# A fused attention and FFT kernel: another list of seeds for its planner, so another order on every engine

## The chip, the cores and the metric

The kernel runs on one core of a Trainium2 chip. A core has five engines that work side by side, each through its own queue in order: TensorE (PE, matrix products; its weight loads are the rows PEld), VectorE (DVE), ScalarE (ACT), GpSimd (POOL) and SyncE (SP, which here issues DMAs only). ACT and POOL issue DMAs too. The engines wait for each other through semaphores. The metric is the device time of one execution in microseconds (us); lower is better.

## The reference

Two branches read the same input x of 2048 rows by 640 and are mixed by a gate of one number per row.

```python
def _A_ref(x, wqkv, wo):                       # H = 32 heads of 20, W, dil = 8, 2
    qkv = (x @ wqkv).reshape(B, S, 3, H, Dh) ...
    idx = pos[:, None] - off[None, :]          # each row sees itself and 7 rows before, every second one
    logits = jnp.einsum("bhsd,bhswd->bhsw", q, kg) * scale
    logits = jnp.where(mask[None, None, :, :], logits, -1e9)
    attn = _softmax(logits, axis=-1)
    o = jnp.einsum("bhsw,bhswd->bhsd", attn, vg)
    return o.reshape(B, S, D) @ wo

def _B_ref(x, w_r, w_i):                       # 2-D FFT, a filter, and back
    X = rfft2(x) * (w_r + 1j * w_i)
    return irfft2(X, s=(S, D))

g = _sigmoid((x * gate_w).sum(-1, keepdims=True))
return g * _A_ref(x, wqkv, wo) + (1 - g) * _B_ref(x, w_r, w_i)
```

## The kernel before

The rows are dealt out as 128 partitions times 16 positions j, so that even and odd positions are two halves ("parities") of the attention, which steps by two rows. Everything is written as a long program of small operations over named tiles:

- **Projections** (`qkv`, tiles `qkv`, `w`, `xe`, `xo`, `ev`). x times wqkv, for 2 parities times 4 groups of heads: eight units u, each of 8 blocks of 15 matmuls with 480 columns (each operand split into a high and a low part, three products for five chunks of the contraction). ACT rounds a weight chunk to its high part (`w<-raw`), POOL or DVE subtracts it from the raw chunk to get the low part. ACT copies each block out of PSUM (`ev<-qkv`) and issues its store to DRAM (`qkvd<-ev`). All of this and the first FFT step share a ring of seven PSUM banks, so the block that takes a bank waits for ACT's copy of the block that had it seven turns before.
- **Attention** (`attend`), 16 units of one parity and two groups of heads' halves. Keys, values and queries are loaded from DRAM (`kt`, `vt`, `q`); ACT copies queries into a PSUM bank (`qbank`); DVE multiplies keys and queries (`pr`) and sums them into `L`; ACT writes a mask into the first partition of L (`L<-low`); DVE takes maxima and sums (`m`, `s`), ACT the exponential; POOL multiplies by the values (`pv`) and DVE sums these into `o`, which is stored to DRAM (`od`).
- **FFT along the columns** (`fold`, `cols`, tiles `fx`, `f`, `z`, `zg`), then the **frequency stage** (`freq`), 16 groups g in the order 1, 2, 3, 0, 4, ... 15: PE makes `v` and `u` from `zc`, DVE their sum and difference (`ab`), PE `x` and `z`. ACT copies x into `P` and sends sign-changed copies `X` of x and z to the other half of the partitions by two DMAs (`P<-X`, the swap). POOL multiplies P by the filter (`P<-P,wp`) and adds, DVE finishes z and writes `s`, PE transforms back into `g`, and ACT writes that into `zg` again.
- **Output projection of the even positions** (`project_even`, tiles `ot`, `oTp`, `oT`, `woa`, `wob`, `ya`), mixed into the frequency stage: PE transposes, ACT and DVE split the result into a high and a low part, PE makes 15 matmuls for each half of the columns, ACT scales by the gate into `ya`.
- **Back to the rows** (`spatial`, tiles `oa`, `ob`, `os`, `ha`, `hb`, `h`, `y`, `yi`), and the **output projection of the odd positions** (`project_odd`), which ends the kernel with a store of half a block.

Nothing is issued in the order in which it is written. `Plan.record` notes each operation with its engine, a modelled busy time and the earlier operations whose data or place it touches. `Plan.order` then makes one order for all engines: `forward` is a list scheduler that takes, of the operations that are ready on an engine, the one with the greatest `tail` (the work still behind it); `backward` runs the plan from its end and gives new tails; `turns` alternates the two and keeps the plan with the earliest modelled end. After that, each number in the list `FOUND` seeds one more move: `move(seed)` draws, for each tile name, kind of tile or kind and engine, a random shift of the tails, the shifts are added to the best tails so far, and two more turns follow. Their best plan becomes the current one. The last plan is issued. All operations are recorded at one line, L608, so the profile tells them apart by their tiles.

Of the kernel before, what the change touches and what calls it, by code (L numbers as in the profile page):

```python
# [156 lines left out]
class Plan:  # L157
# [281 lines left out]

TURNS = 6  # L440
FOUND = (
    300002, 300007, 300009, 300023, 300050, 300094, 300195, 300249, 300251, 300267, 300285, 300341, 300353, 300389, 300427, 300432, 300530, 300592,
    300669, 300713, 301129, 301396, 301423, 301565, 301740, 302062, 302281,
)
ENGS = ("PE", "DVE", "ACT", "POOL", "SP")
RATE = 380e3
# [751 lines left out]
```

## Time and profile before

| | us |
|---|---|
| median of 3 runs | 462.74 |
| lowest and highest run | 460.46, 466.03 |
| span of the profiled execution | 462.3 |

The span runs from the first to the last instruction of the program. A row of busy time gives an engine's share of that span; a row of waits gives the engine and tile that waited, what it waited for, the us in total, how often, and the longest one. In a row of the timeline the number in brackets is the engine's idle time just before, with what ended it. Names such as `P<-X` stand for out<-in. 1,000 ns are 1 us.

### The profile page before, as it was taken

The numbers are of one execution on the slowest core, as the hardware profiler recorded it, in microseconds if no ns is written. First come the engines' busy times: TensorE is split into PE (matmuls) and PEld (weight loads), VectorE is DVE, ScalarE is ACT, GpSimd is POOL, SyncE is SP. The second block draws the span as 40 slices with busy tenths as digits, with TensorE's granted clock in tenths as the row PEclk, the third lists the DMA queues.
The fourth block names the chain that finished last, engine by engine and source line by source line (L and its number), as shares of the span: only waits on it lengthen the run. The fifth ranks groups of instructions, "written<-read, shape, count | busy, mean of one in ns | idle before, by whom it ended". The sixth has DMA issues, their size and how long they took to land. (4 is left out here: it accounts for less than half of the span.)

```text
span 462.3 us, 7218 instructions
## 1 busy us (share of the span) xinstructions
PE 445.6 (96%) x2440; PEld 391.1 (85%) x2440; DVE 408.8 (88%) x522; ACT 213.3 (46%) x558; POOL 340.7 (74%) x284
## 2 busy tenths in 40 slices
PE   9999999999998999999999889998998999999996
PEld 6888888888887888898887668996887889999996
DVE  3999568899999999999989999988999997879575
ACT  4634253543225455254557556665554566342110
POOL 1004355599999889999887898958989999878730
PEclk9999999999998999999999999999999999999999
DMA  8999999669859799759979778888977121364752
GB/s 316 406 399 294 359 382 308 204 198 306 246 165 319 237 268 301 226 167 313 369 213 279 240 257 251 236 271 241 276 233 225 48 67 30 101 210 130 219 195 85
DMA packets 73956, 110.83 MB, mean 240 GB/s; under 512 B 21296, under 2 KB 50992, under 8 KB 73920
## 3 DMA queue, kind: packets, MB, share of 16 engines
q1 hardware_dynamic: 40192, 69.40, 46.9%
q10 hardware_dynamic: 32816, 36.97, 25.7%
q0 software_dynamic: 912, 4.00, 2.2%
q8 instruction: 19, 0.31, 0.3%
q14 instruction: 17, 0.14, 0.1%
HBM read 72.59 MB, written 32.84 MB: 228 GB/s over the span
## 5 line engine op out<-in xcount | busy, mean ns | idle before, releaser
L608 PE MATMUL qkv<-w,xo 128*128 128x480 f32 (+1 forms) x480 | 116.1, 391 | 2.2 <-ACT ev L608 2.2
L608 PE MATMUL qkv<-w,xe 128*128 128x480 f32 (+1 forms) x474 | 104.5, 382 | 0.4 <-POOL w L608 0.4
L608 PEld LDWEIGHTS qkv<-w,xe 128*128 128x128 f32 x474 | 89.1, 189 | 16.0 <-ACT xe L608 0.8
L608 PEld LDWEIGHTS qkv<-w,xo 128*128 128x128 f32 x480 | 89.6, 190 | 15.2 <-ACT ev L608 2.4
L608 ACT COPY ev<-qkv 128x480 f32<-128x480 f32 x64 | 35.2, 557 | 53.6 <-PE qkv L608 32.3
L608 POOL TENSOR_TENSOR P<-P,wp 128x963 f32<-128x963 f32 (+1 forms) x16 | 35.2, 2200 | 13.4 <-DMA P<-X 10.5
L608 PE MATMUL woa<-wo,oT 128*128 128x320 f32 x240 | 42.8, 318 | 1.2 <-DVE oT L608 0.8
L608 PE MATMUL wob<-wo,oT 128*128 128x320 f32 x240 | 41.6, 316 | 0.8 <-ACT ya L608 0.7
L608 POOL TENSOR_TENSOR w<-raw,w 128x480 fp32r<-128x480 f32 (+1 forms) x20 | 25.2, 1273 | 18.2 <-ACT w L608 18.2
L608 PEld LDWEIGHTS woa<-wo,oT 128*128 128x128 f32 x240 | 36.5, 188 | 1.9 <-DVE oT L608 1.3
L608 PEld LDWEIGHTS wob<-wo,oT 128*128 128x128 f32 x240 | 36.3, 188 | 1.7 <-ACT ya L608 1.3
L608 ACT CAST oT<-oTp 128x384 fp32r<-128x384 f32 (+1 forms) x32 | 13.3, 426 | 34.3 <-PE oTp L608 27.4
L608 POOL DMA_DIRECT2D fd<-fx x6 | 4.3, 717 | 33.4 <-DVE fx L608 30.0
L608 PEld LDWEIGHTS g<-mm,s 128*128 128x128 f32 x150 | 21.2, 190 | 6.5 <-ACT zg L608 1.8
L608 PE MATMUL g<-mm,s 128*128 128x128 f32 x150 | 23.8, 278 | 2.4 <-ACT zg L608 1.3
L608 PE MATMUL oa<-gt,zg 128*128 128x161 f32 (+1 forms) x96 | 24.8, 345 | 0.6 <-ACT zg L608 0.6
L608 PE MATMUL ob<-gt,zg 128*128 128x161 f32 (+1 forms) x96 | 23.0, 344 | 0.0
L608 PE MATMUL u<-bt,zc 128*128 128x321 f32 (+2 forms) x96 | 22.7, 345 | 0.1
L608 DVE TENSOR_TENSOR oT<-oTp,oT 128x384 fp32r<-128x384 f32 (+1 forms) x32 | 15.4, 486 | 8.2 <-ACT oT L608 8.0
L608 PE MATMUL v<-bt,zc 128*128 128x321 f32 (+2 forms) x96 | 22.5, 345 | 0.0
L608 PEld LDWEIGHTS z<-fc,f 128*128 128x128 f32 x120 | 17.4, 191 | 2.6 <-DMA f<-fd 1.2
L608 ACT CAST w<-raw 128x480 fp32r<-128x480 f32 (+1 forms) x30 | 17.1, 595 | 4.4 <-PE qkv L608 2.5
(301 smaller groups left out, 1096.9 us busy)
## 6 DMA issues: line engine op xcount, KB each, us to landing
qkvd<-ev ACTq DMA_DIRECT2D x32, 480.0 KB, 5.1
wp<-in_ws SPq DMA_DIRECT2D x16, 642.0 KB, 5.8
raw<-in_wqkv SPq DMA_DIRECT2D x25, 240.0 KB, 7.0
fx<-in_x SPq DMA_DIRECT2D x8, 641.0 KB, 9.1
ot<-od SPq DMA_DIRECT2D x16, 320.0 KB, 3.5
P<-X ACTq DMA_DIRECT2D x30, 160.5 KB, 4.6
fd<-fx POOLq DMA_DIRECT2D x6, 640.0 KB, 7.2
f<-fd SPq DMA_DIRECT2D x6, 640.0 KB, 6.1
```

The source lines that it names most:

```text
L608: p.dve.memset(w, 0.0)
```

## The change

The list of seeds is replaced: 27 numbers before, 65 now. No other line differs; the planner, its costs and the operations stay the same.

```diff
 TURNS = 6
 FOUND = (
-    300002, 300007, 300009, 300023, 300050, 300094, 300195, 300249, 300251, 300267, 300285, 300341, 300353, 300389, 300427, 300432, 300530, 300592,
...
+    800000, 800017, 800030, 800038, 800046, 800064, 800092, 800134, 800297, 800331, 800650, 800739, 800992, 801013, 801073, 801150, 801233, 801252,
...
 )
```

Each engine has the same instructions as before in another order. The stages keep their sequence; what changes is how the attention, the frequency stage and the output projections are woven together, and which small operation stands in front of which. Three places follow. A name such as `ab5_670` is tile ab of group 5, and the number behind the underscore is the tile's own; x2 means twice in a row.

The first place is DVE in the frequency stage, where group 5's `ab` is made, which PE needs for `x5`. Before:

```order
L608 TENSOR_TENSOR pr5a0_536<-kt5a_532,qbank_63 128x1280
L608 TENSOR_TENSOR z3_633<-z3_633,P3_631 128x321
L608 TENSOR_TENSOR t0_659<-z0_647,wp0_636 128x321
L608 TENSOR_TENSOR s3_644<-P3_631,z3_633 128x321
L608 TENSOR_TENSOR s3_644<-P3_631,z3_633 128x319
L608 TENSOR_REDUCE s6a_509<-L6a_503 128x32
L608 RECIPROCAL s6a_509<-s6a_509 128x32
L608 TENSOR_SCALAR ng_74<-g_73 128x16
L608 TENSOR_SCALAR nng_75<-g_73 128x16
L608 TENSOR_TENSOR iz0_658<-iz0_658,wp0_636 128x321
L608 TENSOR_TENSOR iz0_658<-t0_659,iz0_658 128x321
L608 TENSOR_TENSOR ab5_670<-u5_669,vs5_668 128x321 x2
```

In the change:

```order
L610 TENSOR_TENSOR ab5_670<-u5_669,vs5_668 128x321
L610 TENSOR_TENSOR iz0_658<-iz0_658,wp0_636 128x321
L610 TENSOR_TENSOR iz0_658<-t0_659,iz0_658 128x321
L610 TENSOR_TENSOR s0_660<-P0_645,iz0_658 128x321
L610 TENSOR_TENSOR s0_660<-P0_645,iz0_658 128x319
L610 TENSOR_TENSOR ab5_670<-u5_669,vs5_668 128x321
L610 TENSOR_TENSOR pr5a0_536<-kt5a_532,qbank_63 128x1280
L610 TENSOR_REDUCE L6b_519<-pr6b6_523 128x2x8x4
L610 TENSOR_TENSOR ab6_683<-u6_682,vs6_681 128x321 x2
L610 TENSOR_TENSOR oT0_817<-oTp0_818,oT0_817 128x384
L610 TENSOR_REDUCE s6a_509<-L6a_503 128x32
L610 RECIPROCAL s6a_509<-s6a_509 128x32
```

The first of the two ab5 operations now stands ahead of the reduce and reciprocal of s6a, of `ng` (which is the next row after these) and of the product pr5a0; all of those were ahead of it.

The second place is POOL and DVE around group 8 in the same stage. POOL before, with the multiplies by the filter that wait for the swap (`P<-P,wp`), and the attention products pv6a:

```order
L608 TENSOR_TENSOR P7_701<-P7_701,wp7_692 128x963
L608 TENSOR_TENSOR P7_701<-P7_701 128x321
L608 TENSOR_TENSOR pv6a2_512<-vt6a_501,L6a_503 128x8x80 x2
L608 TENSOR_TENSOR P8_714<-P8_714,wp8_705 128x963
L608 TENSOR_TENSOR P8_714<-P8_714 128x321
L608 TENSOR_TENSOR pv6a4_514<-vt6a_501,L6a_503 128x8x80 x2
L608 TENSOR_TENSOR P9_727<-P9_727,wp9_718 128x963
L608 TENSOR_TENSOR P9_727<-P9_727 128x321
```

POOL in the change:

```order
L610 TENSOR_TENSOR P7_701<-P7_701,wp7_692 128x963
L610 TENSOR_TENSOR P7_701<-P7_701 128x321
L610 TENSOR_TENSOR pv6a2_512<-vt6a_501,L6a_503 128x8x80
L610 TENSOR_TENSOR pv6a4_514<-vt6a_501,L6a_503 128x8x80 x2
L610 TENSOR_TENSOR P8_714<-P8_714,wp8_705 128x963
L610 TENSOR_TENSOR P8_714<-P8_714 128x321
L610 TENSOR_TENSOR P9_727<-P9_727,wp9_718 128x963
L610 TENSOR_TENSOR P9_727<-P9_727 128x321
```

The pair pv6a4 now stands ahead of P8, and nothing stands between P8 and P9. DVE before, up to s8, which PE's `g8` reads:

```order
L608 TENSOR_TENSOR oT4_831<-oTp0_832,oT4_831 128x384
L608 TENSOR_TENSOR z8_716<-z8_716,wp8_705 128x321
L608 TENSOR_TENSOR pr5a6_539<-kt5a_532,qbank_63 128x1280
L608 TENSOR_TENSOR oT4_831<-oTp3_833,oT4_831 128x256
L608 TENSOR_TENSOR ab10_737<-u10_736,vs10_735 128x321 x2
L608 TENSOR_REDUCE o6a0_510<-pv6a0_511 128x160
L608 TENSOR_TENSOR z8_716<-z8_716,P8_714 128x321
L608 TENSOR_TENSOR z9_729<-z9_729,wp9_718 128x321
L608 TENSOR_TENSOR s8_726<-P8_714,z8_716 128x321
L608 TENSOR_TENSOR s8_726<-P8_714,z8_716 128x319
```

DVE in the change:

```order
L610 TENSOR_REDUCE L5a_535<-pr5a6_539 128x2x8x4
L610 TENSOR_REDUCE o6a0_510<-pv6a0_511 128x160
L610 TENSOR_TENSOR z8_716<-z8_716,wp8_705 128x321
L610 TENSOR_REDUCE o6a0_510<-pv6a2_512 128x160
L610 TENSOR_TENSOR pr5b0_552<-kt5b_548,qbank_63 128x1280
L610 TENSOR_REDUCE m5a_540<-L5a_535 128x32
L610 TENSOR_TENSOR ab11_750<-u11_749,vs11_748 128x321 x2
L610 TENSOR_TENSOR oT6_838<-oTp0_839,oT6_838 128x384
L610 TENSOR_TENSOR z8_716<-z8_716,P8_714 128x321
L610 TENSOR_REDUCE s6b_525<-L6b_519 128x32
L610 TENSOR_TENSOR s8_726<-P8_714,z8_716 128x321
L610 TENSOR_TENSOR s8_726<-P8_714,z8_716 128x319
```

A reduce into L5a, the second reduce into o6a0, the product pr5b0, ab11 and a part of oT6 now stand ahead of s8; they were behind it.

The third place is ACT and POOL at the turn from the unit qkv7 to qkv6, with the first FFT step (`z0`, `z1`) between them. ACT before; `ev7_6<-qkv7_7` is the copy that frees the bank for the first block of qkv6:

```order
L608 ACTIVATE L2a_407<-L2a_407 128x256
L608 DMA vt2b_421<-qkvd_64 128x1200
L608 COPY L2b_423<-low_80 1x8x2
L608 COPY ev7_6_222<-qkv7_7_223 128x6x80
L608 DMA qkvd_64<-ev7_6_222 128x6x160
L608 COPY L2b_423<-low_80 1x16x4
L608 CAST w1_2_261<-raw1_2_260 128x480
L608 COPY zg_211<-z0_0_234 128x2x256
```

ACT in the change:

```order
L610 ACTIVATE L2a_407<-L2a_407 128x256
L610 COPY L2b_423<-low_80 1x8x2
L610 CAST w1_3_264<-raw1_3_263 128x480
L610 DMA vt2b_421<-qkvd_64 128x1200
L610 COPY zg_211<-z0_0_234 128x2x256
L610 COPY ev7_6_222<-qkv7_7_223 128x6x80
L610 COPY zg_211<-z0_2_235 128x2x256
L610 DMA qkvd_64<-ev7_6_222 128x6x160
```

The first mask of L2b is still ahead of that copy, and a cast of a weight chunk and a copy into zg have come between them. POOL before:

```order
L608 TENSOR_TENSOR pv1a4_386<-vt1a_373,L1a_375 128x8x80 x2
L608 TENSOR_TENSOR L1b_391<-L1b_391,s1b_397 128x256
L608 TENSOR_TENSOR pv1a6_387<-vt1a_373,L1a_375 128x8x80 x2
L608 TENSOR_TENSOR w2_2_229<-raw2_2_228,w2_2_229 128x480
L608 TENSOR_TENSOR L2a_407<-L2a_407,m2a_412 128x256
L608 TENSOR_TENSOR w2_3_231<-raw2_3_230,w2_3_231 128x480
L608 TENSOR_TENSOR w2_4_233<-raw2_4_232,w2_4_233 128x480
L608 TENSOR_TENSOR pv1b0_399<-vt1b_389,L1b_391 128x8x80
```

POOL in the change, some rows earlier in its queue:

```order
L610 TENSOR_TENSOR pv0b0_367<-vt0b_357,L0b_359 128x8x80 x2
L610 TENSOR_TENSOR w2_2_229<-raw2_2_228,w2_2_229 128x480
L610 TENSOR_TENSOR pr1b6_395<-kt1b_388,q1b_390 128x1280
L610 TENSOR_TENSOR w2_3_231<-raw2_3_230,w2_3_231 128x480
L610 TENSOR_TENSOR pv0b2_368<-vt0b_357,L0b_359 128x8x80 x2
L610 TENSOR_TENSOR pv0b4_370<-vt0b_357,L0b_359 128x8x80 x2
```

The subtractions for w2_2 and w2_3 now stand ahead of pr1b6 and of the products pv0b and pv1a, behind which they stood.

More of the change, by code (lines that the diff above doesn't have):

```diff
@@ L441 @@
 FOUND = (
-    300002, 300007, 300009, 300023, 300050, 300094, 300195, 300249, 300251, 300267, 300285, 300341, 300353, 300389, 300427, 300432, 300530, 300592,
-    300669, 300713, 301129, 301396, 301423, 301565, 301740, 302062, 302281,
[4 rows of a table added]
 )
```

3 rows, old and new, of the table FOUND are left out of this document.

## The prediction

> **What bounds the kernel now.** I read first the page's head with its busy shares, then the busy time of each engine in three stretches, then the waits of PE, and last the timeline at the longest of them. The page says how full each engine is:
>
> ```profile
> span 462.3 us, 7218 instructions
> ...
> PE 445.6 (96%) x2440; PEld 391.1 (85%) x2440; DVE 408.8 (88%) x522; ACT 213.3 (46%) x558; POOL 340.7 (74%) x284
> ```
>
> PE is the bound: it is idle for 462.3 - 445.6 = 16.7 us only, and the operations stay the same, so no order gets back more than that and what is hidden inside "busy". The three stretches are the projections to q, k and v, the frequency stage, and the rest:
>
> ```profile
> core 0: us, PE busy (x) PEld busy (x) DVE busy (x) ACT busy (x) POOL busy (x), PEclk, DMA share, GB/s
> 0.00:240.00 240.00, 235.50 (x1134) 203.21 (x1135) 216.42 (x221) 105.82 (x272) 167.80 (x141) 0.99 0.87 287
> 240.00:360.00 120.00, 112.38 (x671) 96.11 (x670) 112.34 (x168) 72.10 (x200) 101.74 (x80) 1.00 0.82 246
> 360.00:462.30 102.30, 97.75 (x637) 91.77 (x636) 80.08 (x136) 35.38 (x87) 71.14 (x65) 0.99 0.39 121
> ```
>
> PE's idle time is 4.5, 7.6 and 4.6 us. The middle stretch is the one to watch: DVE is as full there as PE (7.7 us idle of 120), POOL has 18.3 us free. What ended PE's idle time:
>
> ```profile
> PE qkv L608 <- ACT ev L608: 2.2, 1, 2.2
> PE x L608 <- DVE ab L608: 1.7, 1, 1.7
> PE g L608 <- ACT zg L608: 1.3, 2, 1.0
> PE g L608 <- DVE s L608: 1.1, 1, 1.1
> PE warmed L608 <- DVE warm L608: 1.1, 1, 1.1
> PE oTp L608 <- ACT ya L608: 1.0, 2, 0.8
> PE z L608 <- DMA f<-fd: 0.8, 1, 0.8
> PE woa L608 <- DVE oT L608: 0.8, 1, 0.8
> PE wob L608 <- ACT ya L608: 0.7, 1, 0.7
> PE oa L608 <- ACT zg L608: 0.6, 1, 0.6
> PE oTp L608 <- DVE oT L608: 0.5, 1, 0.5
> PE qkv L608 <- POOL w L608: 0.4, 1, 0.4
> PE woa L608 <- ACT oT L608: 0.4, 1, 0.4
> ```
>
> These are us in total, times, longest. They make 12.6 us; without the first wait for `warm`, which no order removes, 11.5 us. The rest of the 16.7 is mostly the end, which the change leaves as it is (one add and one 160 KB store behind the last matmul in both orders):
>
> ```profile
> 458.71 0.55 DVE y L608
> ```
>
> From 458.7 to 462.3 that is 3.6 us. So 11.5 us is the purse that an order of this kind plays for.
>
> **The change part by part.** All engines and queues are reordered, so I price the places where PE waits, and then what stands newly in front of PE's releasers.
>
> *The wait of 1.7 us, x behind ab (271.2 us).* DVE's row and PE's:
>
> ```profile
> 263.30 1.49 DVE L608 TENSOR_TENSOR pr5a<-kt5a,qbank 128x1280 f32<-128x1280 f32 x1
> 266.30 0.41 DVE L608 TENSOR_REDUCE s6a<-L6a 128x32 f32<-128x256 f32 x1
> 266.74 0.35 DVE L608 RECIPROCAL s6a<-s6a 128x32 f32<-128x32 f32 x1
> 267.01 2.83 DVE L608 TENSOR_SCALAR ng<-g 128x16 f32<-128x16 f32 x1
> 269.74 0.51 DVE L608 TENSOR_TENSOR iz<-iz,wp 128x321 f32<-128x321 f32 x1
> 270.28 0.50 DVE L608 TENSOR_TENSOR iz<-t,iz 128x321 f32<-128x321 f32 x1
> 271.23 0.81 PE L608 MATMUL x<-ab,mm 128*128 128x321 f32 x2 [1.71 <-DVE ab L608]
> ```
>
> The change takes all six of these DVE rows from in front of the first ab5 add: 6.1 us go, and one attention reduce of about 1.4 us comes forward. PE has the same work ahead of x5. The wait goes: -1.7 (ends: 0, if DVE is then held at s3 by POOL's P3 instead, and -1.7).
>
> *The swaps (P8, P9).* A swap is a pair of 160 KB DMAs that POOL's multiply waits for:
>
> ```profile
> 297.40 2.68 POOL L608 TENSOR_TENSOR pv6a<-vt6a,L6a 128x640 f32<-128x640 f32 x2
> 304.29 2.26 POOL L608 TENSOR_TENSOR P<-P,wp 128x963 f32<-128x963 f32 x1 [4.21 <-DMA P<-X]
> 311.81 2.24 POOL L608 TENSOR_TENSOR P<-P,wp 128x963 f32<-128x963 f32 x1 [1.72 <-DMA P<-X]
> ...
> L608 POOL TENSOR_TENSOR P<-P,wp 128x963 f32<-128x963 f32 (+1 forms) x16 | 35.2, 2200 | 13.4 <-DMA P<-X 10.5 <-ACT X L608 2.0 <-ACT oT L608 0.9
> ...
> P<-X ACTq DMA_DIRECT2D x30, 160.5 KB, 4.6
> ...
> 303.93 7.75 DMA P<-X
> ```
>
> Ten of POOL's idle microseconds are this wait; a swap takes 4.6 us in the median and 7.75 us at worst. The Trainium skill (DMA: Bandwidth & Descriptors, the fixed cost of a DMA) gives about 2 us plus the bytes at 436 GB/s; as an estimate that is 2.4 us for 160.5 KB. The trace shows twice to three times that, so the swap is delayed by other transfers here; by the page's price none of these waits would be there at all, and this term would be 0. The change puts both pv6a4 products (2.7 us by the row of their like) before P8 instead of behind it. That fills 2.7 of the 4.2 us in which POOL stood; P8 comes no later, and P9 follows at once, as soon as its own swap has landed. PE sees this through s, in the wait g behind s: 1.1 us. I take half, -0.6 (ends 0, as P9's landing sets it, and -1.1).
>
> *The other waits of order,* 6.5 us by the rows above without the four first and `warm`, less 0.8 for the load of f, which stays: 5.7 us in small pieces. ACT's scaling into ya, which releases 1.7 us of them, stands 0.7 to 4.8 us of work earlier in ACT's queue; the rest are moved by less than 1 us. I take half: -2.9 (ends -5.7 and 0).
>
> *The longest wait, qkv6 behind ev (142.2 us).* The timeline there:
>
> ```profile
> 139.36 2.37 POOL L608 TENSOR_TENSOR w<-raw,w 128x480 fp32r<-128x480 f32 x2
> 140.00 2.88 DVE L608 TENSOR_REDUCE L2b<-pr2b 128x64 f32<-128x1280 f32 x2
> 141.51 0.21 ACT L608 COPY L2b<-low 1x16 f32<-1x16 f32 x1 [1.62 <-DVE L2b L608]
> 141.62 0.54 ACT L608 COPY ev<-qkv 128x480 f32<-128x480 f32 x1
> 142.22 0.48 PE L608 MATMUL qkv<-w,xo 128*128 128x480 f32 x1 [2.19 <-ACT ev L608]
> ...
> 143.60:147.10 3.50, 3.50 (x14) 3.19 (x14) 3.38 (x3) 3.18 (x9) 3.50 (x2) 0.51 1.05 369
> ```
>
> ACT holds the copy that frees PE's bank behind a mask that waits for DVE. In the change the mask is still ahead of it. POOL does two weight subtractions (1.2 us each) before the pv1a products instead of behind them; DVE reads those before it writes L2b, so it loses 2.4 us and wins one reduce of 1.4 us. ACT has a cast, a zg copy and a DMA issue more ahead of ev (about 1.1 us for the first two, by the row of ev). PE has eight matmuls of z1 more to do first (1.8 us). Sum: 2.2 + 2.4 - 1.4 + 1.1 - 1.8 = 2.5 us, so the wait stays: +0.3 (ends -2.2 and +2.4). Behind it PE runs 3.5 us at a granted clock of 0.51, which costs 1.7 us. The Trainium skill (TensorE: Matmul & The Clock Gate, the HAM clock gate) says that the clock is halved after an idle window of about 3.4 us. Here it was halved after 2.2 us idle, so the trace does not hold to that number. By the page the half clock need not come back behind a wait of this length, and the sum would be 1.7 us lower; by the row it comes back, and I leave it in.
>
> *What stands newly in the way.* DVE is the engine without room. Ahead of s8 the change puts 6.8 us of DVE work that stood behind it (four rows of attention at 1.4 to 1.5 us, ab11, a transposed correction, two small ones), while PE gets only 4.1 us more to do before g8 (15 matmuls of wob4 and u12, v12). Ahead of s15 there are two reduces more, 2.9 us, with PE's work unchanged. In part this only fills time in which DVE waited for P. I take +1.3 for both (ends 0 and 2.7 + 2.9 = 5.6). Near the end oT1 gets four small operations and one correction ahead, near 2 us, but DVE is free for 22 of the last 102 us: +0.4 (ends 0 and +2).
>
> Sum: -1.7 - 0.6 - 2.9 + 0.3 + 1.3 + 0.4 = -3.2. The profiled execution spans 462.3 us; the runs shown have 460.46, 462.74 and 466.03, so it stands 0.4 under their median, and I carry nothing across: 462.3 - 3.2 = **459.1 us**.
>
> **The rivals.**
>
> *More than that (453.5).* The new order keeps DVE filled through the whole frequency stage. Its 7.7 us idle less the 2.9 us that are put in front of s15 let the stage end 4.9 us earlier, and the wait at 142 us goes with its half clock (2.2 + 1.7): 462.3 - 8.8 = 453.5. For it: POOL's 18.3 free us in the stage, and attention products moved before P4, P6, P8, P12 and P14. Against it: DVE's idle time is made of many pieces, and my walk through 142 us finds the wait still there. With all 11.5 us and the half clock gone it would be 449.1; no order ends below.
>
> *The order does not matter (462.3).* The waits are set by when transfers land, and these share one memory; the three runs differ by 5.6 us with one and the same order. The waits then only change names. Against it: of PE's 11.5 us just 0.8 ends with a DMA directly.
>
> *Slower (467.9).* DVE comes late: at s8 with 2.7 us, at s15 with 2.9 us, at oT1 with 2, against 1.7 won at x5 and 0.3 of small change: 462.3 + 7.6 - 2.0 = 467.9. It decides from the point where DVE does not use the time in which it stood before, that is, where the stretch from 240 to 360 us still has its 7.7 us of DVE idle time.
>
> **How the numbers follow.** About 1% is what a measurement of this kernel tells from no change, so faster means under 458.1 and slower over 467.4. The forecast has 0.40 and its own range 456 to 462 (0.12 of it faster, 0.28 same); more than that has 0.28, all faster; no effect has 0.15, all same; slower has 0.17, of which 0.02 lies within 1%. That makes faster 0.40, same 0.45, slower 0.15. The range from 451 to 466 leaves out the far end of the first rival (0.04) and most of the last (0.15).
>
> **What would show it.** Right: no wait of x for ab; POOL's wait for P<-X well under 10.5 us; DVE idle under 7.7 us in the frequency stage; PE's idle time near 13 us; still some 2 us for ev before qkv6 and a half clock behind it. Wrong: g waiting for s8 or s15 by 2 us or more, a second half clock, or PE held by a load (f, ot, mm) that had room before.

## The result, and the profile after

| | before | changed |
|---|---|---|
| median, 20 runs each | 463.10 us | 460.99 us |
| lowest and highest run | 460.46, 467.07 | 458.22, 463.34 |
| profiled execution: time | | 461.6 |
| profiled execution: span | 462.3 | 459.7 |
| ratio, 95% interval | | 0.9935 [0.9908, 0.9962] |

The changed kernel is 0.65% faster, which is a little less than the 1% that the prediction counted as a change, and the interval lies wholly under 1. A run's time lies 1.8 to 1.9 us above its span. Ratios, here and below, are against runs of the kernel before on the same chip and leave disturbed runs out, while medians hold all runs; the only profile of h4_early is of a disturbed run (clock 0.852) and isn't read.

The head of the page of the changed kernel, and then its three stretches (busy us of each engine, TensorE's granted clock, share of the DMA engines, GB/s):

```profile
span 459.7 us, 7226 instructions
PE 445.2 (97%) x2440; PEld 389.9 (85%) x2440; DVE 404.7 (88%) x522; ACT 212.6 (46%) x558; POOL 340.6 (74%) x284
```

```profile
0.00:240.00 240.00, 237.41 (x1155) 204.79 (x1156) 218.78 (x225) 108.96 (x279) 171.47 (x145) 1.00 0.87 289
240.00:360.00 120.00, 112.36 (x668) 96.26 (x667) 112.44 (x168) 71.01 (x200) 105.03 (x80) 0.99 0.82 244
360.00:459.70 99.70, 95.42 (x622) 88.87 (x620) 73.50 (x131) 32.68 (x80) 64.12 (x60) 1.00 0.39 122
```

PE's idle time is now 2.6, 7.6 and 4.3 us, where it was 4.5, 7.6 and 4.6. So 1.9 of the 2.6 us come from the projections, 0.3 from the last stretch, 0.4 from busy time, and none from the frequency stage, where most of the prediction's terms lie. In all PE is idle for 14.5 us, where the prediction had near 13. DVE's idle time in the frequency stage is 7.6 us, against 7.7. The longest waits of PE in the changed kernel (us in total, times, longest):

```profile
PE g L610 <- ACT zg L610: 2.3, 5, 0.6
PE v L610 <- ACT vs L610: 1.6, 1, 1.6
PE oTp L610 <- DVE oT L610: 1.4, 1, 1.4
...
PE qkv L610 <- ACT ev L610: 0.3, 1, 0.3
...
PE x L610 <- DVE ab L610: 0.2, 1, 0.2
```

The two longest waits of before, qkv behind ev and x behind ab, are down to 0.3 and 0.2 us, and three that were short or not there stand in their place. POOL's wait for the swaps, from the page's groups, is a third of what it was, though the swaps themselves take longer (5.2 us in the median, 4.6 before):

```profile
L610 POOL TENSOR_TENSOR P<-P,wp 128x963 f32<-128x963 f32 (+1 forms) x16 | 35.3, 2205 | 3.8 <-DMA P<-X 3.6
...
P<-X ACTq DMA_DIRECT2D x30, 160.5 KB, 5.2
```

At the turn to qkv6, the timeline of the changed kernel shows PE without a wait and at full clock:

```profile
141.74 0.46 PE L610 MATMUL qkv<-w,xo 128*128 128x480 f32 x1
```

The half clock has moved to the end of the frequency stage. The timeline of PE and a window there:

```profile
343.06 0.44 PE L610 MATMUL oTp<-ident,ot 128*128 128x128 f32 x2 [1.41 <-DVE oT L610]
344.10 0.71 PE L610 MATMUL g<-mm,s 128*128 128x128 f32 x4 [0.60 <-ACT zg L610]
345.28 1.61 PE L610 MATMUL g<-mm,s 128*128 128x128 f32 x6 [0.46 <-ACT zg L610]
...
344.60:348.10 3.50, 3.04 (x14) 2.85 (x14) 3.41 (x5) 1.21 (x5) 3.42 (x3) 0.61 0.86 265
```

Counted at equal amounts of PE's work in the two traces, the changed kernel is level until 132 us, 3.8 us ahead behind the turn (the wait and the half clock), 5.1 at the end of the projections, 2.5 after the wait of v for vs (244 us), 6.7 at about 264, 3.6 behind the half clock at 348, and 2.6 at the end.

### The profile page after: what moved, and what is told of

It reads as the page before. It is cut to its first block, busy times and chain, and to the rows that moved or that the text cites. A ratio compares the mean times of both kernels' runs of the same rounds, so it can differ in the third digit from the quotient of the medians.

```text
span 459.7 us, 7226 instructions
## 1 busy us (share of the span) xinstructions
PE 445.2 (97%) x2440; PEld 389.9 (85%) x2440; DVE 404.7 (88%) x522; ACT 212.6 (46%) x558; POOL 340.6 (74%) x284
## 4 chain that ended last, share of the span: by engine, by line
PE 77%; DMA 9%; POOL 5%; ACT 3%; DVE 2%; issue 1%; ACTq 1%; SPq 0%; POOLq 0%; DVEq 0%
PE qkv L610 42%; PE wob L610 6%; PE woa L610 5%; PE z L610 5%; PE ob L610 4%; PE oa L610 4%; DMA P<-X 4%; POOL P L610 3%; DMA qkvd<-ev 3%; PE g L610 3%; PE hb L610 2%; PE ha L610 2%; DMA ad<-ya 2%; PE v L610 2%; PE u L610 1%; PE oTp L610 1%
## 5 line engine op out<-in xcount | busy, mean ns | idle before, releaser
L610 PE MATMUL qkv<-w,xo 128*128 128x480 f32 (+1 forms) x480 | 114.1, 387 | 0.0
L610 PE MATMUL woa<-wo,oT 128*128 128x320 f32 x240 | 48.8, 324 | 0.0
L610 PE MATMUL wob<-wo,oT 128*128 128x320 f32 x240 | 47.4, 317 | 1.0 <-ACT oT L610 0.6
L610 PEld LDWEIGHTS wob<-wo,oT 128*128 128x128 f32 x240 | 37.6, 188 | 2.8 <-ACT ya L610 1.6
L610 PEld LDWEIGHTS woa<-wo,oT 128*128 128x128 f32 x240 | 39.0, 193 | 0.8 <-DVE oT L610 0.3
L610 PE MATMUL u<-bt,zc 128*128 128x321 f32 (+2 forms) x96 | 21.6, 345 | 0.0
L610 PEld LDWEIGHTS v<-bt,zc 128*128 128x128 f32 x96 | 15.6, 190 | 4.5 <-ACT vs L610 1.9
```

Of the source, the lines that this page charges most:

```text
L610: p.dve.memset(w, 0.0)
```

## The experiments

Two small additions to the planner make them. One takes single records out of the order and puts them behind others; a record's number is its place in the program as it is written:

```diff
     def issue(self, tc):
         order = self.order()
+        for what, behind in MOVES:
+            op = next(o for o in order if o.i == what)
+            order.remove(op)
+            at = max(n for n, o in enumerate(order) if o.i == behind or o in op.preds) + 1
...
+            order.insert(at, op)
```

The other makes both plans, takes the one up to a cut and then the rest in the other's order:

```diff
...
+    def spliced(self, first, then):
+        cut = next(n for n, op in enumerate(first) if op.i == CUT)
+        done = set(first[:cut])
+        return first[:cut] + [op for op in then if op not in done]
```

### Where the gain is made: the order cut in two

`h1_front` has the change's order up to group 1's first matmul `u1` (about 230 us) and then the order of before; `h2_back` has it the other way round:

```diff
+CUT, SPLICE = 2076, 1     # h1_front
+CUT, SPLICE = 2076, -1    # h2_back
```

> The change's order up to the first matmul of u1 (the end of the projections), the order before for all that is left. Debt theory (what PE wins in front is given back in the frequency stage, since DVE has the same work and no idle time there): the frequency stage loses 2 to 4 us more than before, and the time is 0 to 2.5 us under before. Rival (the change loses at a few rows of its own late order): most of the 5 us won in front stays, the time is 3.5 to 5.5 us under before and 1.5 to 3 us under the change.

> The order before up to the first matmul of u1, the change's order for all that is left. Debt theory: the back is worth nothing or a little by itself, within 1 us of before. Rival (the late order of the change is the worse one): 1.5 to 3.5 us slower than before, with PE waiting for oT of block 12 and a half clock behind it. In both the wait of qkv6 for ev stays near 2 us.

Two earlier cuts followed: at `pv0b0` (104 us in the changed kernel), again from both sides, and at POOL's product of L0a with s0a (79 us).

```diff
+CUT, SPLICE = 1513, 1     # h4_early
+CUT, SPLICE = 1513, -1    # h7_rest
+CUT, SPLICE = 1473, 1     # h6_79
```

> The change's order up to the first product pv0b0 of POOL (103.9 us in the changed kernel's profile), then the order of before. By then the changed kernel's POOL stands 3 us ahead of before's, and one weight subtraction of 1.2 us further. Theory that this lead is all of the front's gain: POOL keeps 2 us or more of it to 135 us, qkv6 waits 0.7 us or less for ev, no half clock follows, and the ratio is that of the front half, 0.992 to 0.995. Rival, that the lead is lost on the way where before's order makes POOL wait for m1a, w and DVE (4.5 us of lead shrank to 0.4 so when the exponential alone was moved): the wait for ev stays 1.5 to 2.2 us, and the ratio is 0.996 to 1.000.

> The change's order up to POOL's product of L0a with s0a (79 us in the changed kernel's profile), then the order of before; the order up to 104 us had given 459.4 us. Theory that the gain lies in the early exponential and s0a: POOL starts L0a with s0a at 79 to 80 us, keeps its lead, qkv6 waits 0.7 us or less for ev, ratio 0.992 to 0.995. Rival, that the order of POOL and DVE between 79 and 104 us is needed too, since before's order has POOL wait there for m0b, w and m1a (3.7 us when the exponential alone was moved): the start is early, the lead at pv0b0 is 1 us or less (before: 107.0 us), the wait for ev is 1.2 to 2.2 us, and the ratio is 0.996 to 1.000.

> The counterpart: before's order up to pv0b0, then the change's to the end. Theory that all of the gain is made ahead of 104 us: the wait for ev at qkv6 is 1.5 us or more, the half clock behind oT12 at 345 to 352 us is there, and the ratio is 1.000 to 1.006, as with the change's order from the first u1 on. Rival, that the order behind pv0b0 brings a part: ratio 0.994 to 0.998.

| kernel | order | median us (before beside it) | ratio, 95% interval | DVE busy, 0 to 100 us |
|---|---|---|---|---|
| before | | 463.1 | 1 | 79.0 |
| h6_79 | change to 79 us, then before | 459.2 (464.9) | 0.9885 [0.9836, 0.9935] | 83.6 |
| h4_early | change to 104 us, then before | 459.4 (462.7) | 0.9936 [0.9909, 0.9963] | |
| h1_front | change to 230 us, then before | 460.7 (463.3) | 0.9931 [0.9906, 0.9956] | 82.3 |
| changed | change throughout | 461.0 (463.1) | 0.9935 [0.9908, 0.9962] | 82.8 |
| h2_back | before to 230 us, then change | 465.9 (463.3) | 1.0027 [0.9995, 1.0059] | 79.3 |
| h7_rest | before to 104 us, then change | 463.8 (464.9) | 0.9994 [0.9966, 1.0022] | 78.9 |

The change's order up to 79 us is enough for the whole gain, and the order behind 104 us shows no gain by itself. h6_79's ratio rests on five runs, and on a chip where the kernel before is slow (464.9); its time is that of h4_early.

The last column is the busy time of DVE in the first 100 us. In the kernels of this table, 3.3 us more of DVE's work done by then goes with a faster kernel. That does not make it the cause. POOL is ahead in the same kernels too, as its first product with L0b shows (before, then h6_79):

```profile
107.04 2.78 POOL L608 TENSOR_TENSOR pv0b<-vt0b,L0b 128x640 f32<-128x640 f32 x2
102.97 2.81 POOL L620 TENSOR_TENSOR pv0b<-vt0b,L0b 128x640 f32<-128x640 f32 x2
```

And two kernels below, e1_exp and e8_wait, do not fit the column.

The forecasts came out only in part. h6_79 has the early start and the lead of POOL that were forecast for the early exponential, with a larger gain than forecast; h4_early's ratio is the one forecast for that lead. By their ratios h1_front and h2_back lie between their two forecasts; h2_back's interval includes 1, though its trace has the wait for oT12 (1.40 us) and the half clock behind it. h7_rest should have waited for ev at qkv6 and had a half clock behind oT12, and did neither. In its trace PE had lost about 4.7 us by 69 us (waits of 2.21 and 0.80 us for weights and 1.7 us by a half clock) and came to the turn 4.4 us later than in the changed kernel, to a bank that was free:

```profile
146.12 0.46 PE L620 MATMUL qkv<-w,xo 128*128 128x480 f32 x1
```

Its span of 461.4 us is no longer than before's 462.3 for that loss. So in this trace PE was not what set the pace up to the turn.

### POOL's late start, one part at a time

In before, POOL starts its first attention products at 86.55 us, in the changed kernel at 79.38, because an exponential on ACT stands behind two copies that wait for a load. `e1_exp` moves only that exponential and the sum and reciprocal behind it; `e2_wsub` moves only POOL's two weight subtractions, which the prediction had counted as a loss:

```diff
+MOVES = ((1470, 573), (1471, 1499), (1472, 1471))   # e1_exp
+MOVES = ((859, 1514), (862, 1578))                  # e2_wsub
```

> The order before, with three rows moved as in the change: ACT's exponential of L0a ahead of the two copies of q1a into qbank (they wait 4.8 us for a DMA), and DVE's s0a pair ahead of pr0b6. Upstream theory (the change wins at the turn to qkv6 because the first attention products start earlier): POOL multiplies L0a by s0a at 79 to 81 us instead of 86.6, the wait of qkv6 for ev falls from 2.2 to under 0.7 us, the half clock behind it goes, and the time falls by 2 to 4 us. Rival (the rows at the turn itself do it): POOL is earlier at 80 us, but the wait of qkv6 stays at 1.5 to 2.5 us and the time is within 0.7 us of before.

> The order before, with POOL's subtractions for w2_2 and w2_3 moved as in the change, ahead of pr1b6 and the products pv0b and pv1a. By the prediction's arithmetic, and by the upstream theory: pv1a comes 2 to 2.5 us later on POOL, L2b is written later on DVE, and the wait of qkv6 for ev grows from 2.2 to 3 to 4.6 us: slower by 1 to 2.5 us. Rival (the rows at the turn do it, these among them): the wait falls under 1 us and the time falls by 1 to 4 us.

e1_exp: 461.74 us against 463.30, ratio 0.9963 [0.9937, 0.9989]. POOL did start early, but the lead was gone 20 us later. POOL's timeline in e1_exp:

```profile
82.02 0.65 POOL L615 TENSOR_TENSOR L0a<-L0a,s0a 128x256 f32<-128x256 f32 x1
89.55 0.63 POOL L615 TENSOR_TENSOR L0b<-L0b,m0b 128x256 f32<-128x256 f32 x1 [1.28 <-DVE m0b L615]
93.86 1.23 POOL L615 TENSOR_TENSOR w<-raw,w 128x480 fp32r<-128x480 f32 x1 [0.61 <-ACT w L615]
100.02 0.63 POOL L615 TENSOR_TENSOR L1a<-L1a,m1a 128x256 f32<-128x256 f32 x1 [1.83 <-DVE m1a L615]
```

It starts 4.5 us earlier and waits 3.7 us, 3.1 of them for DVE: DVE is the late one, and its busy time in the first 100 us is 79.3 us, as in before. At the turn PE still waits:

```profile
142.09 0.48 PE L615 MATMUL qkv<-w,xo 128*128 128x480 f32 x1 [1.96 <-ACT ev L615]
...
143.60:147.10 3.50, 3.50 (x23) 3.19 (x22) 3.37 (x3) 3.18 (x9) 3.50 (x3) 1.00 1.05 376
```

But the wait is 1.96 us and not 2.19, and the clock behind it is full. The time fell by 1.6 us, between the two forecasts (2 to 4 us, and within 0.7 us), and the interval lies under 1. So these three rows bring a part of the gain, though neither POOL's lead nor DVE's work by 100 us explains it in the trace. More runs at full clock explain it only in part. The mean clock is 0.998 or more in 10 of its 12 runs, and in 10 of the 34 of before beside it; among those runs alone its mean time is 462.0 us, against 462.7 for before. How the rest of it comes about is not shown.

e2_wsub: 466.05 us against 463.30, ratio 1.0017 [0.9979, 1.0054]. PE at the turn:

```profile
144.96 0.48 PE L615 MATMUL qkv<-w,xo 128*128 128x480 f32 x1 [4.63 <-ACT ev L615]
...
144.60:148.10 3.50, 3.15 (x12) 2.92 (x13) 3.43 (x5) 2.65 (x8) 2.41 (x1) 0.61 0.95 265
```

The wait grows from 2.19 to 4.63 us, by the 2.4 us of the two subtractions, with a half clock behind it, as the prediction had it. By the ratio the time grows by 0.8 us, and the interval includes 1.

### DVE's idle time ahead of 86 us, one wait alone

The timeline of DVE in before, and of the copies on ACT that it waits for:

```profile
76.26 0.41 DVE L608 TENSOR_REDUCE m0a<-L0a 128x32 f32<-128x256 f32 x1
76.59 1.48 DVE L608 TENSOR_TENSOR pr0b<-kt0b,qbank 128x1280 f32<-128x1280 f32 x1
82.68 1.49 DVE L608 TENSOR_TENSOR pr0b<-kt0b,qbank 128x1280 f32<-128x1280 f32 x1 [3.09 <-ACT qbank L608]
85.61 0.41 DVE L608 TENSOR_REDUCE s0a<-L0a 128x32 f32<-128x256 f32 x1
...
82.02 0.62 ACT L608 COPY qbank<-q1a 128x160 f32<-128x160 f32 x2 [4.77 <-DMA q1a<-qkvd]
```

The same in h6_79:

```profile
72.84 0.41 DVE L620 TENSOR_REDUCE m0a<-L0a 128x32 f32<-128x256 f32 x1
73.17 1.48 DVE L620 TENSOR_TENSOR pr0b<-kt0b,qbank 128x1280 f32<-128x1280 f32 x1
77.48 0.41 DVE L620 TENSOR_REDUCE s0a<-L0a 128x32 f32<-128x256 f32 x1
79.54 1.47 DVE L620 TENSOR_TENSOR pr0b<-kt0b,qbank 128x1280 f32<-128x1280 f32 x1
```

Two things differ in this stretch. The product and reduce of L0b's first quarter stand behind all of L0a, so m0a comes 3.4 us earlier. And the last product pr0b doesn't wait for the copies of q1a. It needs none of them. The kernel uses `qbank` in thirds by turns, and the four copies of q0b were all done by 73.3 us. The program of before nevertheless has it wait for ACT, because the copies of q1a write the other two thirds of the same tile and were issued ahead of it. `e8_wait` takes that wait away. It issues the two copies behind the product, which leaves the order of every engine and queue as it was in before:

```diff
+MOVES = ((1530, 1501), (1533, 1530))
```

> The kernel before, with ACT's first two copies of q1a into qbank issued behind DVE's product pr0b6 in the program, not ahead of it. Every engine and queue keeps before's order to the last instruction; what changes is that pr0b6 no longer waits for those copies, whose bank it doesn't read (3.09 us idle of DVE at 82.7 us in before, since the copies wait for the load of q1a). Theory that DVE sets the pace from about 84 us on, so that what it has done by then is the gain: pr0b6 starts at 79.6 us, DVE is busy for about 27 of the 36 us from 50 to 86 (24.2 in before, 28 to 30 in the kernels that were faster), qkv6 waits for ev 0.8 us or less, no half clock follows in most runs, ratio 0.991 to 0.995. Rival, that POOL's lead or the rest of the front's order made the gain: POOL still starts L0a with s0a at 83 to 86.5 us, the wait for ev stays 1.5 to 2.2 us, ratio 0.997 to 1.001.

DVE in e8_wait, and ACT's copies there:

```profile
76.10 0.41 DVE L615 TENSOR_REDUCE m0a<-L0a 128x32 f32<-128x256 f32 x1
79.34 1.48 DVE L615 TENSOR_TENSOR pr0b<-kt0b,qbank 128x1280 f32<-128x1280 f32 x1
82.25 0.41 DVE L615 TENSOR_REDUCE s0a<-L0a 128x32 f32<-128x256 f32 x1
...
80.85 0.63 ACT L615 COPY qbank<-q1a 128x160 f32<-128x160 f32 x2 [3.76 <-DVE pr0b L615]
```

The edit also turns the wait round: here the copies, and the exponential of L0a behind them, wait for the product.

In the profile everything on DVE and PE followed as the theory has it: s0a 3.4 us earlier, 82.4 us of DVE's work in the first 100 us, no wait at the turn, no half clock, a span of 457.8 us. But the profiled run, 459.62 us, is the fastest of the 12. Their median is 462.35 against 463.09, ratio 0.9989 [0.9965, 1.0013]. The forecast of 0.991 to 0.995 was missed, and the ratio lies in the rival's range of 0.997 to 1.001. By the interval this edit is worth 1.6 us at most. So one trace shows that DVE's wait can lead to PE's wait at the turn, and the runs show that taking it away is not the gain. With all the moves ahead of 79 us, in h6_79, five of six runs lie at 457.5 to 462.8 us.

### Waits inside the frequency stage

`e7_ab5` takes ng and nng from in front of ab5 in the kernel before. `e5_oT` and `e6_vs3` start from the changed kernel and take away its new waits at 343 and 244 us; `b1_both` has both edits.

```diff
+MOVES = ((1422, 2232), (1423, 1422))                  # e7_ab5
+MOVES = ((1905, 2870), (2537, 2869))                  # e5_oT
+MOVES = ((2121, 2149),)                               # e6_vs3
+MOVES = ((1905, 2870), (2537, 2869), (2121, 2149))    # b1_both
```

> The kernel before with one move: DVE makes ng and nng behind the sum and difference ab5, not ahead of them. Theory that each place counts by itself: PE's wait of x for ab, 1.7 us in the profile of before, falls to 0.9 us or less (two instructions of DVE less ahead of it), the waits 2.2 us and the half clock at 142 to 148 us stay; time 0.8 to 1.7 us less, ratio 0.9963 to 0.9983. Rival, that the wait comes back later: ratio 0.9985 to 1.002.

> The changed kernel with two moves at 341 us: DVE sums o6b4 behind, not ahead of, its first subtraction for oT12, and ACT copies the output group of block 12 ahead of, not behind, its two issues of swap P15. PE waited there 1.41 us for oT12, then 0.60 and 0.46 us for that copy and the next, and ran at half clock from 344.5 to 348. Theory that each place counts by itself: the three waits fall from 2.47 us to about 0.6, no half clock follows (1.75 us less), the mean clock is 0.999 or more in most runs, and the time falls from 461.0 by 2 to 3.5 us, ratio to the kernel before 0.987 to 0.991. Rival, that DVE's work in 240 to 360 us (idle 7.6 of 120 us) sets the pace and a wait that is removed comes back a little later: the waits fall here and new ones of the same sum stand before 400 us; the time stays within 0.7 us of 461.0, ratio 0.993 to 0.996.

> The changed kernel with one move at 243 us: ACT copies vs3 right behind the copies of zc0, ahead of two casts of wo4 and of X2's products and swaps, so that v0 need not wait 1.62 us for it; X2's swaps leave 0.4 us later. Theory that each place counts by itself: PE's wait of v for vs falls to 0.3 us or less, the time by 1.0 to 1.7 us from 461.0, ratio to the kernel before 0.990 to 0.992. Rival, that DVE's work sets the pace: the wait moves to x or g within 30 us, and the time stays within 0.7 us of 461.0, ratio 0.993 to 0.996.

> The changed kernel with the three moves of the two kernels before (o6b4 and the copy of block 12's group at 341 us, vs3 at 243 us). Theory that what counts is the half clock, and that a wait removed in the stage comes back in part: no half clock in most runs, 458.0 to 459.5 us, ratio to the kernel before 0.989 to 0.993. If every place counted in full: 461.0 less 2.47, 1.75 and 1.6 is 455 to 456.5 us, ratio 0.983 to 0.987. If nothing was gained: 460 to 461 us, ratio 0.994 to 0.996.

| kernel | median us (before beside it) | ratio, 95% interval | runs with a mean clock of 0.998 or more |
|---|---|---|---|
| e7_ab5 | 463.1 (462.7) | 1.0006 [0.9979, 1.0034] | 10 of 12 |
| changed | 461.0 (463.1) | 0.9935 [0.9908, 0.9962] | 8 of 20 |
| e5_oT | 459.9 (462.7) | 0.9945 [0.9925, 0.9964] | 7 of 8 |
| e6_vs3 | 458.8 (462.7) | 0.9930 [0.9905, 0.9956] | 5 of 7 |
| b1_both | 459.4 (464.9) | 0.9888 [0.9846, 0.9930] | 5 of 6 |

e7_ab5 moved the wait and did not end it. PE and DVE there:

```profile
268.83 0.75 PE L615 MATMUL x<-ab,mm 128*128 128x321 f32 x2
271.25 0.68 PE L615 MATMUL g<-tbfirst,s 128*128 128x128 f32 x4 [1.14 <-DVE s L615]
...
269.36 1.39 DVE L615 TENSOR_SCALAR ng<-g 128x16 f32<-128x16 f32 x1
270.63 0.87 DVE L615 TENSOR_TENSOR s<-P,iz 128x321 f32<-128x321 f32 x2
```

x starts without waiting; g waits 2.4 us later for s, which now has ng and nng ahead of it. No gain is seen from the 1.7 us of before, and by the interval it is 1.0 us at most. The forecast also had the wait of 2.2 us and the half clock at the turn stay. In this profile the wait there is 1.20 us and the clock full, though the order up to that point is before's. In h2_back, again with before's order there, it is 1.75 us. So the 2.19 us of before belong to one execution and not to the order alone.

In e5_oT the three waits at 343 us became 0.58 and 1.05. A new one of 1.49 stood at 310 us; it is 30 us ahead of the rows that were moved, so the edit did not make it:

```profile
310.03 0.91 PE L617 MATMUL g<-mm,s 128*128 128x128 f32 x6 [1.49 <-DVE s L617]
343.38 0.44 PE L617 MATMUL oTp<-ident,ot 128*128 128x128 f32 x2 [0.58 <-DVE oT L617]
345.32 0.94 PE L617 MATMUL g<-mm,s 128*128 128x128 f32 x6 [1.05 <-ACT zg L617]
```

The clock is full in 7 of its 8 runs. That the edit did this is not shown: on the same chip it is full in 16 of 26 runs of before, and in 5 of 7 of e6_vs3, which keeps the three waits. Its 7 runs at full clock have a mean of 459.8 us, the 8 such runs of the changed kernel 459.4: apart from the half clock no gain is seen. In ratio to before it cannot be told from the changed kernel.

e6_vs3 ended the wait for vs, but x waited 0.87 us instead, and its ratio is that of the changed kernel, though its median is 2.2 us lower; this one stays open. b1_both came out at 459.4, inside the range expected where only the half clock counts (458.0 to 459.5) and far above the 455 to 456.5 us of three waits that count in full. h6_79 and b1_both have the lowest ratios here, 1.1% under before, both from the chip on which before is slow (464.9). Their intervals overlap that of the changed kernel, so that they beat it is not shown.

## Why the prediction came out

**The sum was near, and most of its terms were not.** It forecast 3.2 us less; the span fell by 2.6 and the median by 2.1. The forecast of 459.1 was given as a time, though it was worked out from a span, and a time lies 1.9 us above its span. With that it would have been 461.0, which is what was measured (460.99). That it comes so near is luck: terms that were too good and terms that were too bad cancel. The steps, one by one:

- *x behind ab, -1.7.* The wait did fall to 0.2 us. But in e7_ab5, where it was removed alone, the next thing that DVE makes was late and no gain is seen. That agrees with the end of 0 that the prediction named, with s0 as the place and not s3.
- *The swaps, -0.6.* POOL's wait fell from 10.5 to 3.6 us, and PE and DVE idle in the stage as long as before, 7.6 us. That agrees with the end of 0.
- *The other waits of order, half of 5.7.* In the stage the names changed and the sum did not; outside it, 0.3 us came back at the end. Taking a half was a choice without a row behind it. The 6.5 us that it started from are not the rows that the text names: without the four first rows and `warm`, 5.2 of the 12.6 us are left, and 6.5 still holds the row of g behind zg.
- *The turn at qkv6, +0.3.* This is the step that failed. It walked from before's times: POOL has two subtractions more, so DVE, and through it ACT's mask and copy, come later. e2_wsub agrees with this arithmetic as long as the rest stays (4.63 us of wait). But the order further ahead changed too, and the walk left that out: DVE is 3.8 us further by 100 us. In the trace the wait (2.2) and the half clock (1.7) behind it both went, which the prediction had only in a rival. That work done earlier can end the wait is seen in the trace of e8_wait, which has before's order at the turn and no wait there. The row that tells of it, DVE idle for 3.09 us at 82.7 us, is not in the prediction. It watched DVE from 240 us on, but before's DVE is busy for 63.6 of the 64 us from 86 to 150 us already. (The 1.8 us that it gave PE for eight matmuls of z are the price of 16: 36 of them stand ahead of that block in the changed kernel's trace, 20 in before's.)
- *Late work of DVE, +1.3 and +0.4.* g waits for s8 or s15 by no 2 us. Lateness showed in other places: v behind vs 1.6, oTp behind oT12 1.4, and the half clock behind that. Of the 4.1 us that the kernel gave back of its 6.7, most were lost by 348 us.

**The half clock.** The prediction took a half clock of 1.7 us behind a wait of 2.2 us for something that comes back, against the Trainium skill (TensorE: Matmul & The Clock Gate, Part 1), which has the clock fall after an idle window of about 3.4 us. The runs agree with the prediction's row: behind waits of 2.19 and 4.63 us the clock was halved, and in h7_rest, at another place, behind 2.21 us with 0.80 more close by:

```profile
63.72 0.49 PE L620 MATMUL qkv<-w,xe 128*128 128x480 f32 x1 [2.21 <-ACT w L620]
...
64.30:67.80 3.50, 2.79 (x7) 2.37 (x8) 2.40 (x2) 2.61 (x8) 3.50 (x4) 0.56 0.87 225
```

Behind 1.96 (e1_exp) and 1.75 us (h2_back) it was not. Over the 20 runs of the changed kernel, 8 have a mean clock of 0.999 or more and a mean time of 459.4 us, and 11 have 0.995 or 0.996 and 461.4 us. So a half clock, there in about half of the runs, goes with 1.9 us. In the runs of before on the four chips a like split is worth 0.3 to 1.0 us, so the 1.9 are not all the clock's. Nor is the gain a half clock less: in the two profiles it only changed its place.

**The rivals.** "More than that" had its second half right in the trace (the wait at 142 us goes with its half clock) and its first wrong (DVE stays as idle in the stage as it was). "The order does not matter" cannot be told from what the order behind 104 us does (h7_rest, 0.9994). "Slower" was to be decided by DVE's 7.7 us of idle time in the stage. They are still there, and the kernel is faster all the same, by the order ahead of the stage.

**What stays open.** h6_79 shows that the order ahead of 79 us is enough. What in it makes the gain is not shown. The early exponential alone brings a part (e1_exp, 0.9963) without the leads that were to explain it. One wait of DVE removed (e8_wait) gives those leads in its trace and no gain that the runs can tell from none. Which moves make the gain hold from run to run was not taken apart further, and neither was e6_vs3's low median.

## What to carry to other kernels

Where a second engine is nearly full, a wait of the bound engine that it releases may only move when it is removed, as in e7_ab5. Cut a new order in two before explaining it: here the cuts found the place of the gain, ahead of every place that the prediction had priced. Walk a forecast for a place from the new order's start, and not from the old times of what stands in front of it. And do not take a trace for the kernel: e8_wait's span is 4.5 us under before's, and its runs show next to no gain.

## What the runs showed of the hardware

- The margin of the half clock is narrow, and length alone doesn't decide it. In the changed kernel's profile three pieces of idle time (1.41, 0.60 and 0.46 us, with short matmuls between them) halved the clock; the same three places in e6_vs3's profile (1.41, 0.63, 0.46) left it full. Single waits of 1.75 (h2_back) and 1.96 us (e1_exp) left it full, those of 2.19 (before) and 4.63 us (e2_wsub) halved it. Counted from the granted clock in windows of 1 us, each half clock in these traces lasts about 3.4 us, which at half speed costs 1.7 us.
- The median swap took 5.2 us in the changed kernel and 4.6 in before, while POOL waited 6.9 us less for swaps: the swaps didn't get faster. In the order shown for P8, other work of POOL stands ahead of the multiply instead.
